# First batch's scores as plain f32 products, and the table of distances scaled on GpSimd

## The chip, the cores and the metric

The kernel runs on one core of a Trainium2 chip. A core has TensorE (matrix products into PSUM), VectorE, ScalarE and GpSimd (elementwise work) and SyncE, whose queue (SP) issues all of this kernel's DMAs. The metric is the device time of one execution in microseconds. Before the change the median of three runs is 654.57 us (652.57 to 655.28).

## What is computed

Windowed attention with a linear bias for 8 batches of 8 heads (576 positions, head width 64), and behind it a mixing layer over positions and channels. Cut to what matters:

```python
scores = scale * np.matmul(q, k.transpose(0, 1, 3, 2))      # scale = 1/8
bias   = slopes[:, None, None] * (-np.abs(rel))[None]       # slopes 2^-(h+1), rel = query - key position
mask   = (rel >= 0) & (rel < 128)
scores = np.where(mask, scores + bias[None], -1e9)
attn   = softmax(scores)
x      = np.matmul(attn, v)                                 # heads side by side: (B, 576, 512)
theta  = x @ w_theta
zr, zi = x * cos(theta), x * sin(theta)
u      = x + w_tok_r @ zr + w_tok_i @ zi                    # over positions
out    = u + relu(u @ w_ch)
```

All arrays are float32.

## The kernel before, in words

The 64 heads are worked in 32 pairs, two heads at a time: head 2p lies in array rows and partitions 0 to 63, head 2p+1 in 64 to 127. Pairs 0 to 3 are batch 0. A pair's scores come in three groups of tiles (`SCORES`): tile 0 alone (both heads' last 64 queries in one product of 192 columns, `mm`), tiles 1 and 2 (128 and 256 columns per head), tiles 3 and 4 (256 and 256 per head, `ps`). Each tile holds only the keys of the window.

To keep f32 precision the kernel splits q and k into a high part of the type f32r and a low rest, also f32r: `split_high` has ScalarE write `qh` (q times a power of two and -1/8) and `kh`; `split_low` has VectorE write `ql` = q - qh and GpSimd `kl` = k - kh. The scores are the sum of three products, qh kh, ql kh and qh kl. `weigh` is one VectorE instruction per tile and head: scores from PSUM times a power of two plus the table of distances (`bands`, a constant from the host with both heads' slopes; the power of two turns it to the pair's slopes), with the row's minimum taken along; ScalarE follows with the exponential in place (`front`, `back`). For the first four pairs (`PLAIN = 4`) the attention weights are turned by TensorE in f32 (`flip`, into PSUM, copied out as `pt` by ScalarE) and multiplied with plain f32 values (`ps<-vb,pt`); from pair 4 on f16 parts and DMA transposes do this.

While the first batch's attention runs (`start`), the weights are unpacked: 4 chunks of w_theta and 9 of w_tok arrive as pairs of 32-bit words (u_hi, u_lo, xtf, z_hi and z_lo are the buffers that they pass through), and `unpack` turns each into high and low parts: ScalarE (`apart`, L168, L169), VectorE (`together`, L174, L176), ScalarE and VectorE again (`split`, and for w_tok a row scale, L181 to L193). `pace` mixes these steps with the scores.

The order on each engine's queue is set by a scheduler that models time and moves instructions within their dependencies; the queues themselves run in order. Buffers come from pools: `qk` has two buffers for each of qh, kh, ql and kl, so a pair's tile reuses the one of the pair two before it. q and k are loaded into `qr` and `kr` (one buffer each); pair 1 borrows a buffer of the values (`vb`). GpSimd clears the unused corner of q's tile first. `prepare(p)` splits pair p-1 and loads pair p.

## Time and profile before

| what | value |
|---|---|
| median of the runs | 654.57 us |
| the profiled execution, its own time | 654.73 us |
| its span, first to last instruction | 652.7 us |
| TensorE busy | 604.9 us (93%) |
| VectorE busy | 529.3 us (81%) |
| ScalarE busy | 499.0 us (76%) |
| GpSimd busy | 145.7 us (22%) |
| mean granted TensorE clock | 0.963 |
| DMA traffic | 79.16 MB, mean 121 GB/s |

In the profile a time is counted from the start of the span. PE is TensorE, DVE VectorE, ACT ScalarE, POOL GpSimd. The share of busy time is a mean over stages of different kinds: the change lies in the first 65 us, and that stage has to be read by itself. A duration in a timeline row can overlap with the next instruction's; what an instruction takes from its engine is the distance from its start to the next start. The granted clock is a share of full speed, 1.00 being 2.4 GHz and 0.50 being 1.2 GHz.

### The profile page before, as it was taken

Reading aid. Unit: us, or ns where it says so; the run is one execution under the profiler, and the core shown is the slowest. Engines: PE = TensorE matmul, PEld = TensorE weight load, DVE = VectorE, ACT = ScalarE, POOL = GpSimd, SP = SyncE. Lnnn points to the kernel's source line nnn. Section 1 sums busy time; section 2 is a strip of 40 time slices with the busy share of each in tenths; the row PEclk is TensorE's granted clock in tenths of the full one; section 3 lists DMA queues with packets and bytes.
Section 4 is the critical chain, followed back from the end, with each engine's and each line's share of the span. In section 5 each row is a group of like instructions: output and inputs, shape, how many; then the busy total and the mean of one; then the engine's idle time right before and its main releaser. Section 6 shows DMA issues by size and latency. Waiting matters only on the chain.

```text
span 652.7 us, 14918 instructions
## 1 busy us (share of the span) xinstructions
PE 604.9 (93%) x5712; PEld 520.5 (80%) x5712; DVE 529.3 (81%) x1313; ACT 499.0 (76%) x945; POOL 145.7 (22%) x196
## 2 busy tenths in 40 slices
PE   4869888689999999999999999999999999999998
PEld 3758666578887898789878887889878988799887
DVE  4998799797799778988799878997899878946612
ACT  6999879785987668976988778786898799727710
POOL 3001001542213202222203302231212212210220
PEclk9567999798999899999999999999999999999999
DMA  9954412996038740698039920887058901631001
GB/s 267 338 176 123 106 25 59 210 200 147 27 79 199 173 109 21 143 199 188 23 75 197 211 70 20 188 176 171 28 104 197 183 28 41 136 83 38 19 19 56
DMA packets 149096, 79.16 MB, mean 121 GB/s; under 512 B 122144, under 2 KB 138528, under 8 KB 149024
## 3 DMA queue, kind: packets, MB, share of 16 engines
q1 hardware_dynamic: 149024, 78.21, 51.6%
q8 instruction: 45, 0.74, 0.5%
q14 instruction: 27, 0.22, 0.1%
HBM read 39.39 MB, written 9.44 MB: 75 GB/s over the span
## 4 chain that ended last, share of the span: by engine, by line
PE 59%; DVE 18%; ACT 12%; DMA 9%; issue 2%; SPq 0%; POOL 0%; ACTq 0%; DVEq 0%; POOLq 0%
PE mm L73 47%; PE ps L73 9%; DMA pt<-hl 7%; PE ps L88 2%; ACT front L436 2%; ACT back L436 2%; DVE hl L452 2%; DMA qr<-in_qt_dram 2%; ACT hl L450 2%; DVE g L568 1%; DVE f L568 1%; DVE x_sb L490 1%; ACT L436 1%; DVE z_lo L513 1%; DVE fixed L141 1%
## 5 line engine op out<-in xcount | busy, mean ns | idle before, releaser
L73 PE MATMUL mm<-wtk_hi,z_lo 128*128 128x288 f16 x576 | 166.2, 289 | 6.4 <-DVE z_lo L513 5.5
L73 PE MATMUL mm<-wtk_hi,z_hi 128*128 128x288 f16 x576 | 166.8, 290 | 0.5 <-ACT z_hi L512 0.5
L73 PE MATMUL mm<-wtk_lo,z_hi 128*128 128x288 f16 x576 | 166.2, 289 | 0.0
L73 PEld LDWEIGHTS <-z_hi 128*128 128x128 f16 x1152 | 108.1, 99 | 31.1 <-ACT z_hi L512 0.8
L642 POOL TENSOR_TENSOR u_lo<-xtf,u_hi 128x288 fp32r<-128x288 f32 x64 | 54.6, 868 | 137.6 <-DVE vl L370 95.2
L349 POOL TENSOR_TENSOR kl<-kr,kh 128x576 fp32r<-128x576 f32 x31 | 44.0, 1418 | 154.6 <-issue 80.7
L73 PEld LDWEIGHTS <-z_lo 128*128 128x128 f16 x576 | 56.9, 99 | 26.0 <-DVE z_lo L513 10.5
L436 ACT ACTIVATE front<-front,fixed 128x256 f32<-128x256 f32 (+2 forms) x160 | 60.4, 444 | 14.2 <-DVE fixed L433 13.9
L73 PE MATMUL ps<-vh,pt 128*128 128x65 f16 x1008 | 54.6, 198 | 12.6 <-DMA pt<-hl 10.6
L73 PEld LDWEIGHTS <-pt 128*128 128x128 f16 x1512 | 52.7, 100 | 15.3 <-DMA pt<-hl 12.8
L452 DVE SCALAR_TENSOR_TENSOR hl<-front,hl 128x1024 f16<-128x1024 f32 x28 | 51.4, 1837 | 9.4 <-ACT hl L450 9.3
L436 ACT ACTIVATE back<-back,fixed 128x256 f32<-128x256 f32 x128 | 57.2, 494 | 0.4 <-DVE fixed L433 0.4
L640 ACT CAST u_hi<-xtf 128x288 fp32r<-128x288 f32 x64 | 27.0, 423 | 38.9 <-DVE xtf L638 38.9
L73 PE MATMUL ps<-vl,pt 128*128 128x64 f16 x504 | 52.3, 196 | 0.0
L73 PE MATMUL mm<-u_hi,wch_hi 128*128 128x288 f32 x256 | 47.9, 309 | 0.0
L433 DVE CUSTOM_DVE_ANT_0 back<-ps,bands 128x256 f32<-128x256 f32 x128 | 46.8, 419 | 1.1 <-PE ps L73 1.1
L638 DVE SCALAR_TENSOR_TENSOR xtf<-mm,fixed,xtf 128x288 f32<-128x288 f32 x64 | 32.4, 509 | 18.8 <-PE mm L73 18.8
L73 PE MATMUL mm<-wth_hi,x_hi 128*128 128x512 f32 x160 | 46.4, 412 | 0.9 <-DVE x_hi L530 0.9
L73 PE MATMUL ps<-kh,qh 64*128 64x256 f32 (+1 forms) x256 | 41.7, 321 | 5.2 <-DVE x_sb L490 3.9
L670 DVE SCALAR_TENSOR_TENSOR xtf<-mm,xtf 128x288 f32<-128x288 f32 x64 | 29.1, 454 | 20.8 <-PE mm L73 20.0
L73 PE MATMUL mm<-u_hi,wch_lo 128*128 128x288 f32 x256 | 44.5, 295 | 0.0
L73 PE MATMUL mm<-u_lo,wch_hi 128*128 128x288 f32 x256 | 44.4, 295 | 0.0
(162 smaller groups left out, 1487.4 us busy)
## 6 DMA issues: line engine op xcount, KB each, us to landing
vb<-in_vx_dram SPq DMA_DIRECT2D x16, 650.0 KB, 5.7
out_dram<-xtf SPq DMA_DIRECT2D x64, 144.0 KB, 1.8
kr<-in_kt_dram SPq DMA_DIRECT2D x31, 288.0 KB, 3.9
qr<-in_qt_dram SPq DMA_DIRECT2D x31, 144.0 KB, 2.9
qr<-in_qt_dram SPq DMA_DIRECT2D x31, 128.0 KB, 3.1
xtf<-in_wch_dram SPq DMA_DIRECT2D x4, 512.0 KB, 4.2
z_hi<-in_wtok_dram SPq DMA_DIRECT2D x2, 576.0 KB, 6.0
z_lo<-in_wtok_dram SPq DMA_DIRECT2D x2, 576.0 KB, 6.2
```

Of the source, the lines that this page charges most:

```text
L73: ins = nc.tensor.matmul(*args, **kw)
L88: ins = nc.tensor.transpose(*args)
L349: rest = nc.gpsimd.tensor_tensor(out=kl, in0=kr, in1=kh.bitcast(F32), op=ALU.subtract)
L433: self.weighed = nc.vector.tensor_tensor_reduce(out=sb, in0=ps, in1=bias, scale=2.0 ** -(2 * self.p % H + 1), scalar=3.0e38, op0=ALU.add, ...
L436: self.exps.append(nc.scalar.activation(sb, sb, AF.Exp, bias=least, scale=-1.0))
L450: self.copied = nc.scalar.activation(hl[:, 0], src, AF.Copy, scale=2.0 ** PEXP)
L452: self.lowered = nc.vector.scalar_tensor_tensor(out=hl[:, 1], in0=src, scalar=2.0 ** PEXP, in1=hl[:, 0], op0=ALU.mult, op1=ALU.subtract)
L568: nc.vector.scalar_tensor_tensor(out=z, in0=x_sb[:, i, :], scalar=zs[:, c:c + 1], in1=z, op0=ALU.mult, op1=ALU.mult)
L638: nc.vector.scalar_tensor_tensor(out=xtf[:, m, cs], in0=y_ps[:, :HALF], scalar=st["back"], in1=xtf[:, m, cs], op0=ALU.mult, op1=ALU.add)
L640: nc.scalar.copy(u_hi[:, m, cs], xtf[:, m, cs])
L642: return nc.gpsimd.tensor_tensor(out=u_lo[:, m, cs], in0=xtf[:, m, cs], in1=u_hi[:, m, cs].bitcast(F32), op=ALU.subtract)
L670: nc.vector.scalar_tensor_tensor(out=xtf[:, e, cs], in0=o_ps[:, :HALF], scalar=0.0, in1=xtf[:, e, cs], op0=ALU.max, op1=ALU.add)
```

## The change

For pairs 0 to 3 q and k are used as they are loaded: four plain f32 buffers per pair (named qh, kh, ql and kl, from the same pool) hold q, k and the table of distances in two pieces (512 and 192 columns). `split_pair` hands them through, and each score product is one f32 product in place of three f32r ones. The factor -1/8 moves into `weigh`, whose power of two for the pair's slopes moves into the table: the host's table is multiplied by -4, pair 0's comes by DMA straight into its buffers, and GpSimd makes the table of pair p from that of pair p-1 by a factor 0.25 (`distances`), and from pair 3's the one that all later pairs use, `bands`, by a factor -16. q's corner is cleared per pair on GpSimd. Pairs 4 and later are computed as before.

```diff
--- before.py
+++ after.py
@@ -127,9 +127,12 @@
     sums, rows, invs, lim = (rings[name].take() for name in ("sum", "row", "inv", "lim"))
 
     qr = const.tile([128, S + 64], F32, name="qr")
-    second = vbp.tile([128, GROUP, NT, 65], F32, name="vb").rearrange("p h c d -> p (h c d)")
-    qr_too, kr_too = second[:, :S + 64], second[:, S + 64:2 * S + 64]
-    for t in [qr, qr_too] + peaks + [front[:, 192:256] for front in fronts]:
+    def plain_buffers():
+
+        return [qk.tile([128, w], F32, name=name) for name, w in (("qh", S + 64), ("kh", S), ("ql", S + 64), ("kl", S))]
+
+    plain = [plain_buffers() for _ in range(2)]
+    for t in [p[0][:, 512:] for p in plain] + [front[:, 192:256] for front in fronts] + peaks + [qr]:
         nc.gpsimd.memset(t, 0.0)
 
     ORDER = (0, 4, 1, 5, 2, 6, 3, 7, 8)
@@ -232,7 +235,13 @@
 
     def load_pair(p):
         b, h = divmod(2 * p, H)
-        q, kr = (qr_too, kr_too) if p == 1 else (qr, ld.tile([128, S], F32, name="kr"))
+        if p < PLAIN:
+            if p >= 2:
+                plain.append(plain_buffers())
+                nc.gpsimd.memset(plain[p][0][:, 512:], 0.0)
+            q, kr = plain[p][:2]
+        else:
+            q, kr = qr, ld.tile([128, S], F32, name="kr")
         nc.sync.dma_start(out=q[:64, :S], in_=qt[b, h])
         nc.sync.dma_start(out=q[64:, :512], in_=qt[b, h + 1, :, :512])
         nc.sync.dma_start(out=q[64:, S:], in_=qt[b, h + 1, :, 512:])
@@ -329,7 +338,17 @@
         nc.vector.tensor_copy(fixed[:, c:c + GROUP], scale[:, 9:13])
 
     def split_pair(p, raw):
-        return split_low(split_high(p, raw))
+        return raw if p < PLAIN else split_low(split_high(p, raw))
+
+    def distances(p):
+
+        if p == 0:
+            nc.sync.dma_start(out=plain[0][2][:, :512], in_=band[:, :512])
+            nc.sync.dma_start(out=plain[0][3][:, :192], in_=band[:, 512:])
+            return
+        parts = (bands[:, :512], bands[:, 512:]) if p == PLAIN else (plain[p][2][:, :512], plain[p][3][:, :192])
+        for to, of in zip(parts, (plain[p - 1][2][:, :512], plain[p - 1][3][:, :192])):
+            nc.gpsimd.tensor_scalar(out=to, in0=of, scalar1=-16.0 if p == PLAIN else 0.25, scalar2=None, op0=ALU.mult)
 
     def split_high(p, raw):
 
@@ -389,6 +408,8 @@
             self.p = p
             self.terms = parts.pop(p)
             self.early = p < PLAIN
+            self.bias = ((plain[p][2], plain[p][3]) if self.early else (bands, bands[:, 512:]))
+            self.scale = -0.125 if self.early else 2.0 ** -(2 * p % H + 1)
             self.heads = [Head(2 * p + e, self) for e in range(2)]
             self.mx = rings["mx"].take().rearrange("p (e i) -> p e i", e=2)
             self.pt, self.exps = {}, []
@@ -396,13 +417,14 @@
 
         def scores(self, tiles, behind=None):
 
-            last = len(self.terms) - 1
+            terms = (self.terms,) if self.early else self.terms
+            last = len(terms) - 1
             if tiles == (0,):
                 _, _, k0, kn, _ = TILES[0]
                 ps = ps_m.tile([128, 512], F32, name="mm")
-                for j, (qm, km) in enumerate(self.terms):
+                for j, (qm, km) in enumerate(terms):
                     mm(ps[:, :kn], qm[:, 512:], km[:, k0:k0 + kn], start=(j == 0), stop=(j == last))
-                self.weigh(0, 0, self.src[0][:, :kn], ps[:, :kn], bands[:, 512:], behind)
+                self.weigh(0, 0, self.src[0][:, :kn], ps[:, :kn], self.bias[1][:, :kn], behind)
                 return
             ps = ps_s.tile([128, 2, 512], F32, name="ps")
             if tiles == (1, 2):
@@ -413,7 +435,7 @@
             off = 0
             for i in tiles:
                 q0, qn, k0, kn, _ = TILES[i]
-                for j, (qm, km) in enumerate(self.terms):
+                for j, (qm, km) in enumerate(terms):
                     for e in range(2):
                         rows = slice(64 * e, 64 * e + 64)
                         mm(ps[:, e, off:off + kn], qm[rows, q0:q0 + qn], km[rows, k0:k0 + kn],
@@ -424,13 +446,13 @@
                 _, _, _, kn, c0 = TILES[i]
                 for e in range(2):
                     sb = sbs[e][:, off:off + kn]
-                    self.weigh(i, e, sb, ps[:, e, off:off + kn], bands[:, 256 * e + c0:256 * e + c0 + kn], behind)
+                    self.weigh(i, e, sb, ps[:, e, off:off + kn], self.bias[0][:, 256 * e + c0:256 * e + c0 + kn], behind)
                 off += kn
 
         def weigh(self, i, e, sb, ps, bias, behind):
 
             least = self.mx[:, e, i:i + 1]
-            self.weighed = nc.vector.tensor_tensor_reduce(out=sb, in0=ps, in1=bias, scale=2.0 ** -(2 * self.p % H + 1),
+            self.weighed = nc.vector.tensor_tensor_reduce(out=sb, in0=ps, in1=bias, scale=self.scale,
                                                           scalar=3.0e38, op0=ALU.add, op1=ALU.min, accum_out=least)
             with tc.issue_after(behind.ins) if behind is not None else nullcontext():
                 self.exps.append(nc.scalar.activation(sb, sb, AF.Exp, bias=least, scale=-1.0))
@@ -758,8 +780,9 @@
 
         next(load)
         prepare(0)
-        nc.sync.dma_start(out=bands, in_=band)
+        distances(0)
         prepare(1)
+        distances(1)
         last = None
         for p in range(H // 2 + 1):
             new = Pair(p)
@@ -790,6 +813,8 @@
             if p in (1, 2):
                 measure(p - 1, peaks[0][:, GROUP * (p - 1):GROUP * p])
             prepare(p + 2)
+            if 2 <= p + 2 <= PLAIN:
+                distances(p + 2)
             last = new
         for _ in load:
             pass
@@ -850,7 +875,7 @@
     split = np.where((rel >= 0) & (rel < WINDOW), rel.astype(np.float32), np.float32(-NEG * 256))
     half = split * 0.5
     last = np.concatenate([split[:64, :192], half[:64, :192]], axis=0)
-    return np.concatenate([split, half, last], axis=1).astype(np.float32)
+    return (-4.0 * np.concatenate([split, half, last], axis=1)).astype(np.float32)
 
 
 def _layout(q, k, v, moe_w_theta, moe_w_tok_r, moe_w_tok_i, moe_w_ch):
```

On TensorE, from the second turning of pair 0's weights (back) to the products with pair 0's values (vb,pt); ps and mm are products in PSUM, L88 is a turning, L73 a product, + is the changed kernel and - the one before:

```order
 L88 MATMUL ps<-fixed,back 128x128 x8
+L73 MATMUL ps<-kh,qh 128x256 x4
+L73 MATMUL ps<-vb,pt 128x65 x18
 L73 MATMUL mm<-kh,qh 128x192
-L73 MATMUL mm<-kh,ql 128x192
-L73 MATMUL ps<-kh,qh 128x256 x2
-L73 MATMUL ps<-kh,ql 128x256 x2
-L73 MATMUL ps<-kl,qh 128x256 x2
-L73 MATMUL ps<-kh,qh 128x256 x2
-L73 MATMUL ps<-kh,ql 128x256 x2
-L73 MATMUL ps<-kl,qh 128x256 x2
-L73 MATMUL mm<-kl,qh 128x192
```

Two f32 products per head stand for six f32r ones, and the values of pair 0 now come ahead of pair 2's tile 0 (mm).

On GpSimd, from the last fill ahead of the loop to the first fills of vh (the values' parts), before:

```order
L133 MEMSET front_102 128x64
L369 MEMSET vh 128x5
L349 TENSOR_TENSOR kl<-kr,kh 128x576
L349 TENSOR_TENSOR kl<-vb,kh 128x576
L349 TENSOR_TENSOR kl<-kr,kh 128x576 x4
L369 MEMSET vh 128x5 x4
```

and in the changed kernel, where ql and kl of pairs 1 to 3 are the two pieces of the table and the qh fills are the corners of q for pairs 2 and 3:

```order
L388 MEMSET vh 128x5
L351 TENSOR_SCALAR ql<-ql 128x512
L351 TENSOR_SCALAR kl<-kl 128x192 x2
L241 MEMSET qh 128x128
L351 TENSOR_SCALAR ql<-ql 128x512
L351 TENSOR_SCALAR kl<-kl 128x192
L351 TENSOR_SCALAR bands<-kl 128x192
L241 MEMSET qh 128x128
L351 TENSOR_SCALAR ql<-ql 128x512
L351 TENSOR_SCALAR bands<-ql 128x512
L368 TENSOR_TENSOR kl<-kr,kh 128x576 x2
```

Four subtractions of 576 columns give way to eight scalings, six of them behind pair 1's own two.

On the SP queue, from the second chunk of w_tok to the fourth (z_lo to u_lo), before, where the q and k in qr and kr are pair 3's:

```order
L158 DMA z_lo<-in_wtok_dram 128x1152
L245 DMA vb<-in_vx_dram 128x4x325
L253 DMA vb<-in_vx_dram 128x4x325
L158 DMA u_hi<-in_wtok_dram 128x1152
L158 DMA u_lo<-in_wtok_dram 128x1152
L236 DMA qr<-in_qt_dram 64x576
L237 DMA qr<-in_qt_dram 64x512
L238 DMA qr<-in_qt_dram 64x64
L239 DMA kr<-in_kt_dram 128x576
```

and in the changed kernel, where qr and kr are pair 4's and qh and kh pair 2's:

```order
L254 DMA vb<-in_vx_dram 128x4x325
L245 DMA qr<-in_qt_dram 64x576
L246 DMA qr<-in_qt_dram 64x512
L247 DMA qr<-in_qt_dram 64x64
L246 DMA qh<-in_qt_dram 64x512
L245 DMA qh<-in_qt_dram 64x576
L247 DMA qh<-in_qt_dram 64x64
L248 DMA kh<-in_kt_dram 128x576
L248 DMA kr<-in_kt_dram 128x576
L262 DMA vb<-in_vx_dram 128x4x325
L161 DMA u_hi<-in_wtok_dram 128x1152
L161 DMA u_lo<-in_wtok_dram 128x1152
```

The loads of pairs 2 and 4 stand ahead of these two chunks now; before, pair 2's stood ahead of xtf, z_hi and z_lo, and pair 4's far behind.

## Rows read from the trace of the kernel before

**Rows 1.** Busy time by stretch (window: length, busy us per engine, clock, DMA share, GB/s).

```profile
20.00:30.00 10.00, 9.52 (x47) 8.89 (x48) 9.86 (x28) 10.00 (x21) 1.42 (x1) 0.50 1.05 354
30.00:40.00 10.00, 6.56 (x35) 6.11 (x36) 9.74 (x20) 10.00 (x21) 1.46 (x1) 0.50 0.47 145
40.00:50.00 10.00, 7.04 (x43) 6.21 (x40) 9.55 (x30) 10.00 (x21) 0.88 (x1) 0.67 0.55 197
50.00:60.00 10.00, 9.15 (x61) 8.59 (x62) 9.07 (x27) 10.00 (x22) 0.67 (x1) 0.69 0.58 174
```

**Rows 2.** Timeline of ScalarE (start us, us, engine, line, operation, out<-in, shape, count).

```profile
12.32 0.69 ACT L168 ACTIVATE u_lo<-u_lo 128x512 f32<-128x512 f32 x1
...
14.46 0.66 ACT L168 ACTIVATE xtf<-xtf 128x512 f32<-128x512 f32 x1
...
15.59 0.49 ACT L436 ACTIVATE front<-front,fixed 128x256 f32<-128x256 f32 x1
...
31.41 0.72 ACT L168 ACTIVATE u_lo<-u_lo 128x576 f32<-128x576 f32 x1
...
32.65 0.73 ACT L340 ACTIVATE qh<-qr 128x640 fp32r<-128x640 f32 x1
...
33.84 0.78 ACT L192 ACTIVATE wtk_hi<-z_hi,fixed 128x576 f16<-128x576 f32 x1
```

**Rows 3.** Timeline of the SP queue, loads of weight chunks.

```profile
7.09 0.33 SPq L158 DMA_DIRECT2D u_lo<-in_wth_dram  x1
7.68 0.33 SPq L158 DMA_DIRECT2D xtf<-in_wth_dram  x1
...
19.31 0.34 SPq L158 DMA_DIRECT2D u_lo<-in_wtok_dram  x1
```

**Rows 4.** DMA issues up to 90 us: count, KB each, us to landing.

```profile
xtf<-in_wth_dram SPq DMA_DIRECT2D x2, 512.0 KB, 6.6
...
u_lo<-in_wtok_dram SPq DMA_DIRECT2D x1, 576.0 KB, 10.1
...
u_lo<-in_wth_dram SPq DMA_DIRECT2D x1, 512.0 KB, 5.2
```

**Rows 5.** Timeline of VectorE.

```profile
12.15 0.29 DVE L433 CUSTOM_DVE_ANT_0 front<-ps,bands 128x128 f32<-128x128 f32 x1
...
19.80 0.82 DVE L347 SCALAR_TENSOR_TENSOR ql<-qr,qh 128x640 fp32r<-128x640 f32 x1
20.53 0.28 DVE L433 CUSTOM_DVE_ANT_0 front<-ps,bands 128x128 f32<-128x128 f32 x1
...
34.21 1.95 DVE L347 SCALAR_TENSOR_TENSOR ql<-qr,qh 128x640 fp32r<-128x640 f32 x1
36.08 0.75 DVE L176 SCALAR_TENSOR_TENSOR u_lo<-u_lo 128x576 int32<-128x576 int32 x1
```

**Rows 6.** Timeline of GpSimd.

```profile
2.26 0.30 POOL masks.py:199 TENSOR_SCALAR_AFFINE_SELECT fixed<-fixed 128x128 f32<-128x128 f32 x1
...
11.96 1.51 POOL L349 TENSOR_TENSOR kl<-vb,kh 128x576 fp32r<-128x576 f32 x1 [3.22 <-ACT kh L341]
...
34.02 1.46 POOL L349 TENSOR_TENSOR kl<-kr,kh 128x576 fp32r<-128x576 f32 x1 [11.84 <-ACT kh L341]
```

**Rows 7.** GpSimd's groups by form (busy us, mean ns of one, idle before).

```profile
L642 POOL TENSOR_TENSOR u_lo<-xtf,u_hi 128x288 fp32r<-128x288 f32 x64 | 54.6, 868 | 137.6 <-DVE vl L370 95.2 <-ACT u_hi L640 35.2 <-ACT vh L368 3.7
...
L197 POOL TENSOR_TENSOR wch_lo<-xtf,wch_hi 128x512 fp32r<-128x512 f32 x4 | 5.4, 1343 | 4.7 <-ACT wch_hi L196 4.7
...
L133 POOL MEMSET qr<- 128x640 f32 x1 | 0.6, 637 | 0.0
```

**Rows 8.** Timeline of TensorE.

```profile
22.43 0.58 PE L73 MATMUL ps<-kh,qh 64*128 64x256 f32 x2
...
24.01 0.53 PE L73 MATMUL mm<-kl,qh 128*128 128x192 f32 x1
24.86 7.94 PE L73 MATMUL ps<-vb,pt 128*128 128x65 f32 x36 [0.32 <-ACT pt L445]
```

## The prediction, made before the changed kernel ran

> **What bounds the kernel now.** I read the core's summary first, then busy time in stretches of 10 us, then the timelines of ScalarE, VectorE, GpSimd, TensorE and the SP queue up to 80 us, because the diff touches only the first batch's four pairs. In the four stretches from 20 to 60 us ScalarE is busy 10.00 of 10 each time and VectorE 9.86, 9.74, 9.55 and 9.07, so VectorE has 1.78 us of idle time in 40; TensorE has 7.73 us and GpSimd nearly all of it [rows 1]. The stretch is an exchange between two full engines: ScalarE and VectorE unpack the 13 weight chunks and, between them, weigh the scores and take the exponentials of pairs 0 to 4. TensorE has slack there, although its clock was granted at 0.50 to 0.69. Whatever comes off both full engines comes off the end of the stretch, and everything later shifts with it: from the first token mixing on, no engine's order changes. So the whole question is how much of the first 65 us goes.
>
> **The change part by part.**
> ScalarE loses qh and kh of four pairs. Pair 3's two stand from 32.65 to 33.84, so 1.19 us a pair and 4.76 us in all [rows 2].
>
> Not all of that is gained. The first two weight chunks behind pair 1's loads are taken as they land: u_lo is issued at 7.09 and takes 5.2, so it lands at 12.29, and ScalarE starts on it at 12.32; xtf lands at 7.68 + 6.6 = 14.28 and is started at 14.46 [rows 2 to 4]. These loads don't come sooner (the table of distances is now two transfers, which puts them one issue later if anything). With 2.38 us of copies gone before 14.46, ScalarE can only bring forward one exponential of 256 columns, which stood behind xtf at 15.59 (0.49 us), and the 0.18 us to the landing [rows 2]. That is 0.67 of 2.38; 1.71 us turn into waiting. ScalarE's net is 4.76 - 1.71 = 3.05 us.
>
> VectorE loses ql of four pairs. Pairs 0 and 1 come while it still waits for weight chunks to land, and count as nothing. Pair 2's costs 20.53 - 19.80 = 0.73, pair 3's 36.08 - 34.21 = 1.87, together 2.60 us [rows 5].
>
> Pair 3's is that long because GpSimd was writing kl from 34.02 to 35.48 [rows 6]: the VectorE instruction began at 34.21 and ended 0.68 us after GpSimd did, that is, it stood until GpSimd was through. Weighing, which takes its scores from PSUM, does not stand: at 12.15, inside kl of pair 1 (11.96, 1.51 us), it took its usual 0.29 [rows 5, 6]. The Trainium skill has this as a rule ("SBUF — State Buffer", section "Who interferes with whom"): a VectorE instruction with two SBUF inputs and a GpSimd instruction that reads SBUF exclude each other for the whole instruction, one with at most one SBUF input is free. The trace agrees in both halves, with the 1.87 and the 0.29. By that rule the new scalings, which read SBUF, stop VectorE just as kl did, and with every one of them stopping it the VectorE term below would be 2.60 - 3.12, a small loss instead of a small gain.
>
> GpSimd loses four kl and gains four scalings of 512 columns and four of 192, two of them for pair 1, before VectorE is busy; the other six fall between 15 and 30 us. No row shows a scaling. From below, by a plain fill of 640 columns in 0.637 us, about 1.0 ns a column, 512 and 192 columns cost 0.51 and 0.19, six of them 2.1 us. From above, by two-operand subtractions, 1.343 for 512 columns and 0.868 for 288 (more than 192 can cost), they cost 6.6 us [rows 7]. The nearest row is the one-operand select of 128 columns, 0.30 us [rows 6]; with the fill's 1.0 ns for further columns that gives 0.68 and 0.36, 3.12 us for six, which I take. VectorE reads two SBUF operands in about two thirds of this stretch, my estimate, so 2.0 of 3.12 stop it. VectorE's net is 2.60 - 2.0 = 0.6 us.
>
> TensorE does one f32 product in place of three f32r ones. The only plain f32 products in the trace are those with the values: 18 of them appear as 36 weight loads and products in 7.94 us at the half clock, 0.221 us each [rows 8]. A pair's scores are 9 products, so 18 of these: 3.97 us at the half clock, if the columns (65 there, up to 256 here) add nothing. With three f32r parts two tiles of 256 columns take from 22.43 to 24.01, 1.58 us, so a pair some 3.9 [rows 8]. From below the change is then about nothing. From above, with time in proportion to columns, one f32 product part of 256 columns would take 0.221 x 256/65 = 0.87 us and a pair some 13.4, 9.5 more. I take +0.5 us a pair, near the lower end, because in the nearest products of the same shape the two heads (array rows 0 to 63 and 64 to 127) run side by side: 12 parts of 256 columns in that 1.58 us, 0.13 each, where one alone would need more. TensorE's 7.73 us of idle time hide it; without that cover it costs 2 us. The skill states ("FP8 and Floating Point Precision", section "TensorE Precision Notes") that true f32 takes four passes. No run here separates passes; by four in place of three a pair would take an estimated 1.3 us more at the half clock, and 3 pairs in that clock 3.9, still inside the idle time.
>
> The waits that are added: TensorE starts on pair 0 when q and k land, not after ScalarE's copy, which helps by under 1 us and then waits for the table. GpSimd's fills of the q tiles for pairs 2 and 3 now stand behind scalings that wait for VectorE's weighing, and the SP queue's loads stand behind those fills: pair 3's load holds back the two xtf chunks. Those are needed only after 35 us, so I cost that at nothing.
>
> **Sum.** ScalarE could end 3.05 us earlier, VectorE 0.6. Neither can run ahead of the other for long, since each chunk passes back and forth between them; I take the middle, 1.8 us. The profiled execution took 654.73, 0.16 above the median of 654.57. Forecast: 654.57 - 1.8 = 652.8 us, with a range of its own from 654.0 (0.6) to 651.5 (3.05).
>
> **Rivals.**
> A, more is gained. Pair 2's q and k no longer stand ahead of the first unpacking loads, so chunks land sooner, and the scalings fall beside weighing, which they don't stop. Then ScalarE's 4.76 us count nearly whole: 650.2. For it speaks ScalarE's zero idle time in rows 1; against it, that u_lo and xtf are still the first loads behind pair 1's.
> B, f32 products of 64 rows don't run side by side. Pairs 1 to 3 in the cold clock each need 16 more part times of 0.221, 3.5 us, together 10.6; half of it covered by TensorE's idle time, 5.3 stays: 654.6 - 1.8 + 5.3 = 658.1. The f32r rows speak against it.
> C, the change of places in the SP queue eats the gain. Pair 4's q and k (576 KB) now go out ahead of the second round of weight loads. At the 354 GB/s of 20 to 30 us that is 1.7 us; u_lo, issued at 19.31 and 10.1 us on its way, landed at 29.41 and was used at 31.41 [rows 1 to 4]. Now it lands near 31.1, while ScalarE wants it some 2 us sooner than before. It waits 1.7 us, and what is left is about nothing: 654.4.
> D, slower through GpSimd. If the six scalings cost what two-operand subtractions do, 6.6 us, and all stop VectorE, it loses 6.6 - 2.6 = 4.0, of which its 1.78 us of idle time hide part: 654.6 + 2.2 = 656.8. It decides from the point where the blocked time exceeds 2.60 + 1.78 = 4.4 us. That the rule on shared access holds in this trace speaks for it; that a scaling reads one operand, against it.
>
> **How the numbers follow.** Forecast 0.46, A 0.20, C 0.18, D 0.10, B 0.06. Half a per cent, about what a measurement can tell from no change, is 3.3 us: faster is below 651.3, slower above 657.8. Faster: most of A and the edge of the forecast, 0.22. Slower: B and a third of D, with what I have not seen, 0.11. The rest, 0.67, is within. The range takes in most of A and up to D: 650.0 to 656.6.
>
> **What would show it.** Right: ScalarE busy under 10 of 10 between 10 and 20 us, with waits for the landing of u_lo and xtf; scalings of 512 columns near 0.7 us with VectorE's two-operand rows stretched beside them; the last exponentials of pair 3 some 2 us sooner; nothing different after the first token mixing but the shift. A pair's 256-column tile near 0.9 us at the half clock or 0.45 at the full one says that the heads run side by side; twice that is B. A wait of ScalarE for u_lo near 30 us is C. I am wrong in the mechanism if ScalarE and VectorE gain idle time of over 4 us between 20 and 60 us and TensorE is what they wait for.

## Result: slower by 0.8%, and where in the profile it stands

The changed kernel takes 659.48 us (median of 20 runs, 654.83 to 661.39) against 653.03 us of the kernel before in as many runs beside it. The medians stand 6.4 us apart; the ratio, which goes by the means, is 1.0084 (5.5 us), with a 95% interval of 1.0065 to 1.0104. The forecast was 652.8 us. The profiled execution took 659.62 us, its span is 657.8. In the runs further down, single executions of over 2500 us count in a median and not in a ratio.

Busy time by stretch, the kernel after (columns as in [rows 1]):

```profile
10.00:20.00 10.00, 7.06 (x36) 5.08 (x35) 7.67 (x26) 8.74 (x18) 5.97 (x7) 0.82 1.03 385
20.00:30.00 10.00, 8.56 (x40) 7.34 (x38) 10.00 (x29) 8.48 (x19) 2.12 (x2) 0.50 1.04 300
30.00:40.00 10.00, 9.21 (x40) 7.33 (x41) 9.55 (x28) 9.86 (x18) 1.51 (x2) 0.50 0.94 309
40.00:50.00 10.00, 8.57 (x48) 8.08 (x49) 9.83 (x22) 10.00 (x22) 1.55 (x1) 0.67 0.35 107
50.00:60.00 10.00, 7.72 (x34) 5.38 (x32) 8.15 (x29) 10.00 (x22) 0.00 (x0) 0.50 0.47 150
60.00:70.00 10.00, 9.02 (x43) 9.03 (x44) 5.01 (x13) 3.48 (x8) 1.57 (x4) 0.50 0.22 61
```

Up to 60 us it reads much as forecast: ScalarE has some idle time ahead of 40 us, VectorE gains little. The row that is new is the last. ScalarE is busy for 3.48 of 10 us, TensorE for 9.02, at a granted clock of 0.50. Before, the same stretch had ScalarE at 8.40 and the clock at 1.00:

```profile
60.00:70.00 10.00, 8.65 (x86) 7.80 (x84) 7.37 (x35) 8.40 (x18) 1.53 (x4) 1.00 0.21 60
```

ScalarE's timeline names what it waits for; after first, then before:

```profile
61.76 1.72 ACT L458 ACTIVATE back<-back,fixed 128x256 f32<-128x256 f32 x4
70.66 1.01 ACT L467 COPY pt<-ps 128x1024 f32<-128x1024 f32 x1 [7.18 <-PE ps L88]
```

```profile
62.39 1.70 ACT L436 ACTIVATE back<-back,fixed 128x256 f32<-128x256 f32 x4
65.69 1.01 ACT L445 COPY pt<-ps 128x1024 f32<-128x1024 f32 x1 [1.60 <-PE ps L88]
```

ScalarE ends pair 3's exponentials at 63.48 instead of 64.09, so 0.6 us of the gain did reach this point. Then it waits 7.18 us for TensorE's turning of pair 3's probabilities, where it waited 1.60. TensorE's timeline from there, after:

```profile
42.53 6.92 PE L73 MATMUL ps<-vb,pt 128*128 128x65 f32 x36 [1.43 <-ACT pt L467]
...
51.68 1.65 PE L73 MATMUL ps<-kh,qh 64*128 64x128 f32 x8
55.43 1.97 PE L88 MATMUL ps<-fixed,back 128*128 128x128 f32 x8 [2.10 <-ACT pt L467]
57.33 2.08 PE L73 MATMUL ps<-kh,qh 64*128 64x256 f32 x8
59.34 0.47 PE L88 MATMUL mm<-fixed,peak 128*128 128x128 f32 x1
60.98 7.94 PE L73 MATMUL ps<-vb,pt 128*128 128x65 f32 x36 [1.16 <-DVE fixed L455]
68.71 1.91 PE L88 MATMUL ps<-fixed,front 128*128 128x128 f32 x8
```

And before:

```profile
46.34 7.95 PE L73 MATMUL ps<-vb,pt 128*128 128x65 f32 x36 [2.70 <-DVE fixed L433]
54.08 1.91 PE L88 MATMUL ps<-fixed,front 128*128 128x128 f32 x8
...
58.03 1.09 PE L88 MATMUL ps<-fixed,back 128*128 128x128 f32 x8 [0.60 <-ACT pt L445]
...
60.54 4.23 PE L73 MATMUL ps<-vb,pt 128*128 128x65 f32 x36
64.61 1.04 PE L88 MATMUL ps<-fixed,front 128*128 128x128 f32 x8
```

At 55.43 the changed kernel is 2.6 us ahead (the back turning began at 58.03 before). Then the same 36 rows of pair 2's values take 7.94 us instead of 4.23, and the turning 1.91 instead of 1.04. Both go with the clock. Busy time in stretches that are all at one clock, before and then after:

```profile
47.00:56.00 9.00, 9.00 (x45) 9.00 (x44) 7.65 (x13) 9.00 (x19) 1.55 (x1) 0.50 0.55 170
57.00:95.00 38.00, 32.34 (x228) 26.74 (x226) 31.27 (x87) 30.55 (x57) 1.53 (x4) 1.00 0.29 69
```

```profile
45.00:73.00 28.00, 24.74 (x118) 22.15 (x119) 20.08 (x61) 20.82 (x44) 3.11 (x5) 0.50 0.31 97
75.00:84.00 9.00, 5.19 (x48) 4.75 (x45) 4.95 (x13) 5.69 (x9) 0.00 (x0) 1.00 0.34 65
85.00:87.00 2.00, 2.00 (x5) 1.61 (x6) 1.98 (x4) 1.81 (x4) 0.00 (x0) 0.50 1.00 164
```

Before, the clock rose to 1.00 (2.4 GHz) at 56.3 us, after ten microseconds in which TensorE did not pause. In the changed kernel it stayed at 0.50 (1.2 GHz) until 74.4 and fell again from 84.6 to 88.0, in the first theta products. (The instants are read from windows of 1 us.)

From pair 2's values to the first mixing product (91.77 before, 100.81 after) the 9.0 us come together as follows, each the difference of two distances between starts: start of the values 0.4 (60.98 against 60.54); the values 3.7; from there to pair 3's values 1.7; to the first theta product 1.8; the theta products 1.4. The third, fourth and fifth follow from starts at 64.61, 70.05 and 77.29 before and 68.71, 75.82 and 84.91 after. Second and third stand at half clock but for the end of the third, and the last has its first 3.1 us there; together they are 6.8 us. The fourth stands at full clock and is a wait for VectorE, 3.27 us where it was 1.03:

```profile
83.66 0.77 PE L88 MATMUL ps<-fixed,x_sb 128*128 128x128 f32 x5 [3.27 <-DVE x_sb L512]
```

The two profiled executions differ by 4.9 (the medians by 6.4), so some 4 of the 9.0 are given back later: before has three later spells at half clock, from 121.1, 148.4 and 213.3 us, 13.6 us in all; after has one, from 129.0, of 6.8. The lower clock is not one of the profiled execution alone: over the changed kernel's 20 runs the mean granted clock is 0.944 to 0.958 (median 0.950), in the kernel before's runs beside the experiments 0.955 to 0.992 (medians 0.963 to 0.976).

### The profile page after: what moved, and what is told of

Read it like the earlier page. It is cut to its first block, busy times and chain, and to the rows that moved or that the text cites. A ratio compares the mean times of both kernels' runs of the same rounds, so it can differ in the third digit from the quotient of the medians.

```text
span 657.8 us, 14837 instructions
## 1 busy us (share of the span) xinstructions
PE 610.6 (93%) x5676; PEld 523.1 (80%) x5676; DVE 525.4 (80%) x1309; ACT 494.4 (75%) x937; POOL 148.6 (23%) x203
## 4 chain that ended last, share of the span: by engine, by line
PE 63%; DVE 14%; ACT 11%; DMA 10%; issue 2%; POOL 0%; SPq 0%; ACTq 0%; POOLq 0%; DVEq 0%
PE mm L73 49%; PE ps L73 11%; DMA pt<-hl 6%; PE ps L88 3%; ACT back L458 2%; DVE hl L474 2%; ACT front L458 2%; ACT hl L472 1%; DVE g L590 1%; DVE f L590 1%; DMA u_lo<-in_wtok_dram 1%; DVE z_lo L535 1%; ACT L458 1%; DVE fixed L144 1%; DMA kr<-in_kt_dram 1%
## 5 line engine op out<-in xcount | busy, mean ns | idle before, releaser
L73 PE MATMUL mm<-wtk_hi,z_lo 128*128 128x288 f16 x576 | 165.0, 287 | 6.5 <-DVE z_lo L535 5.5
L73 PE MATMUL mm<-wtk_hi,z_hi 128*128 128x288 f16 x576 | 165.4, 287 | 0.5 <-ACT z_hi L534 0.5
L73 PE MATMUL mm<-wtk_lo,z_hi 128*128 128x288 f16 x576 | 164.9, 286 | 0.0
L73 PEld LDWEIGHTS <-z_hi 128*128 128x128 f16 x1152 | 107.3, 98 | 30.3 <-ACT z_hi L534 0.8
L664 POOL TENSOR_TENSOR u_lo<-xtf,u_hi 128x288 fp32r<-128x288 f32 x64 | 53.4, 850 | 139.6 <-DVE vl L389 81.4
L73 PEld LDWEIGHTS <-z_lo 128*128 128x128 f16 x576 | 56.4, 98 | 25.4 <-DVE z_lo L535 10.5
L368 POOL TENSOR_TENSOR kl<-kr,kh 128x576 fp32r<-128x576 f32 x28 | 39.7, 1418 | 132.0 <-issue 80.6
L73 PE MATMUL ps<-vh,pt 128*128 128x65 f16 x1008 | 53.3, 196 | 11.8 <-DMA pt<-hl 10.2
L73 PEld LDWEIGHTS <-pt 128*128 128x128 f16 x1512 | 51.4, 99 | 14.6 <-DMA pt<-hl 12.1
L73 PE MATMUL ps<-kh,qh 64*128 64x256 f32 (+1 forms) x288 | 49.5, 374 | 5.7 <-DVE fixed L455 3.8
L73 PE MATMUL ps<-vl,pt 128*128 128x64 f16 x504 | 51.0, 194 | 0.0
L73 PE MATMUL mm<-wth_hi,x_hi 128*128 128x512 f32 x160 | 47.3, 418 | 1.0 <-DVE x_hi L552 1.0
L73 PE MATMUL mm<-u_hi,wch_hi 128*128 128x288 f32 x256 | 47.8, 308 | 0.0
L73 PE MATMUL mm<-u_hi,wch_lo 128*128 128x288 f32 x256 | 44.5, 295 | 0.0
L73 PE MATMUL mm<-u_lo,wch_hi 128*128 128x288 f32 x256 | 44.4, 295 | 0.0
L73 PE MATMUL mm<-wth_lo,x_hi 128*128 128x512 f32 x160 | 44.3, 399 | 0.0
```

The lines of the kernel that those rows point to most:

```text
L73: ins = nc.tensor.matmul(*args, **kw)
L368: rest = nc.gpsimd.tensor_tensor(out=kl, in0=kr, in1=kh.bitcast(F32), op=ALU.subtract)
L664: return nc.gpsimd.tensor_tensor(out=u_lo[:, m, cs], in0=xtf[:, m, cs], in1=u_hi[:, m, cs].bitcast(F32), op=ALU.subtract)
```

## Experiments

Theory 1: the loss is TensorE's clock in this tail. Theory 2: it is GpSimd's scalings, or the loads that now wait on SP's queue. Each run has the kernel before beside it on the same chip, but the runs come from several chips, so rows are compared by their ratios rather than their medians; "half clock" sums the time at 0.50 in the first 100 us of its profile, "values" is the start and length of pair 2's.

| run | half clock | values | first mixing product | median | ratio, 95% interval |
|---|---|---|---|---|---|
| before | 34.2 | 60.54, 4.23 | 91.77 | 653.03 | |
| after | 58.0 | 60.98, 7.94 | 100.81 | 659.48 | 1.0084 (1.0065, 1.0104) |
| e1_f32_only | 40.9 | 62.21, 4.23 | 94.96 | 652.03 | 0.9989 (0.9966, 1.0012) |
| e2_f32r_still | 68.4 | 62.37, 7.95 | 105.29 | 664.77 | 1.0179 (1.0147, 1.0211) |
| e3_warm | 54.5 | 60.12, 5.76 | 95.78 | 656.12 | 1.0057 (1.0027, 1.0087) |
| e4_no_scalings | 58.0 | 59.72, 7.94 | 99.84 | 658.30 | 1.0080 (1.0053, 1.0107) |
| e5_warm_more | 30.6 | 59.27, 4.23 | 91.41 | 652.41 | 0.9994 (0.9974, 1.0014) |
| e6_three_plain | 64.9 | 63.09, 8.05 | 103.45 | 665.66 | 1.0202 (1.0179, 1.0225) |
| e7_gpsimd_loads | 37.6 | 61.67, 4.23 | 94.43 | 654.10 | 1.0023 (0.9999, 1.0046) |
| e8_both | 40.9 | 65.35, 4.15 | 97.42 | 658.86 | 1.0107 (1.0080, 1.0135) |
| e12_before_hole | 44.4 | 63.88, 4.23 | 94.36 | 654.69 | 1.0054 (1.0021, 1.0088) |
| five14 | 51.2 | 60.67, 7.08 | 98.06 | 657.90 | 1.0094 (1.0059, 1.0128) |
| tail13 | 32.7 | 59.48, 4.23 | 91.34 | 651.07 | 0.9969 (0.9950, 0.9987) |
| before15 | 40.9 | 62.49, 4.13 | 95.17 | 656.78 | 1.0060 (1.0038, 1.0082) |

**The plain f32 product alone.** The kernel before, with the f32 product in `scores`:

```diff
+            if self.early:
+                qh, kh = self.terms[0]
+                self.terms = ((qh.bitcast(F32), kh.bitcast(F32)),)
```

> The kernel before, with pairs 0 to 3's scores as one plain f32 product of qh and kh instead of three f32r products; every split is still made, and the low parts are left out of these pairs' scores. TensorE does what it does in the changed kernel; ScalarE, VectorE, GpSimd and SP's queue do what they do before. Theory 1 (the loss is TensorE's granted clock: 0.50 from 43.7 to 74.4 us in the changed kernel, from 46.0 to 56.3 before): slower than before by 3 to 6 us, 656 to 659 us, pair 2's values of x36 at 7.9 us as in the changed kernel and not 4.2. Theory 2 (GpSimd's six scalings and the loads behind them on SP's queue make the loss): within 1 us of before, 652 to 654 us, values of pair 2 at 4.2 us.

652.03 us, level with the kernel before, as theory 2 had it; pair 2's values at 62.21 take 4.23. Theory 1 as first put, that f32 score products keep the clock low, is out: TensorE had the changed kernel's products, and the clock rose at 58.8, after a stretch like that of before:

```profile
47.42 7.94 PE L73 MATMUL ps<-vb,pt 128*128 128x65 f32 x36 [1.09 <-ACT pt L448]
55.16 1.91 PE L88 MATMUL ps<-fixed,front 128*128 128x128 f32 x8
...
58.04 1.30 PE L73 MATMUL ps<-kh,qh 64*128 64x128 f32 x8 [0.38 <-DVE fixed L183]
59.26 1.10 PE L88 MATMUL ps<-fixed,back 128*128 128x128 f32 x8
```

The last row starts with no wait; after the change this turning has 2.10 us of waiting for ScalarE ahead of it.

**The f32r products, with the rest of the change.** A constant tile takes the place of q and k:

```diff
-            terms = (self.terms,) if self.early else self.terms
+            terms = (None,) * 3 if self.early else self.terms     # None: still[:, :128], still[:, :kn]
```

> The changed kernel, with pairs 0 to 3's scores as three f32r products of one constant tile, as many and as wide as before the change; what it leaves out is q and k themselves in these scores. TensorE does what it does before; loads, scalings and the missing splits are the changed kernel's. Theory 1 (clock): the full clock is back by about 57 us, pair 2's values take about 4.2 us, and the time is at or under the kernel before, 649 to 653 us. Theory 2 (scalings and queue): still slow, 657 to 660 us.

664.77 us, the other way from what theory 1 said. With f32r products the clock stays low even longer. So f32r score products alone do not bring the clock back. TensorE's waits are there, too:

```profile
45.57 7.95 PE L73 MATMUL ps<-vb,pt 128*128 128x65 f32 x36 [2.47 <-ACT pt L475]
...
58.34 1.60 PE L88 MATMUL ps<-fixed,back 128*128 128x128 f32 x8 [1.93 <-DVE fixed L463]
...
62.37 7.95 PE L73 MATMUL ps<-vb,pt 128*128 128x65 f32 x36 [0.85 <-ACT pt L475]
```

The clock did rise, at 55.3, and fell at 58.7, behind the wait of 1.93 us.

**No scalings.** All pairs share one table:

```diff
-        for to, of in zip(parts, ...):
-            nc.gpsimd.tensor_scalar(out=to, in0=of, scalar1=..., op0=ALU.mult)
+            nc.sync.dma_start(out=bands[:, :512], in_=band[:, :512])       # p == 0 only
```

> The changed kernel without GpSimd's scalings of the table: pairs 0 to 3 and all later ones share one table, loaded once; what it leaves out is the pairs' own slopes (and the sign of the scores) in pairs 0 to 3. Theory 1 (clock): little changes, 657 to 660 us, pair 2's values still at 7.9 us. Theory 2 (about 7 us of scalings on GpSimd): 652 to 654 us.

658.30 us, ratio 1.0080 (1.0053 to 1.0107) against 1.0084: the scalings are not the loss.

**Work put into TensorE's waits.** `warm(n)` issues n products nobody reads, behind the last TensorE instruction:

```diff
+    def warm(n):
+        ps = ps_m.tile([128, 512], F32, name="mm")
+        with tc.issue_after(latest_pe[0].ins):
+            for k in range(n):
+                mm(ps, wth_hi[:, k % 4, :128], wth_hi[:, (k + 1) % 4, :], start=(k == 0), stop=(k == n - 1))
                 scores(SCORES[1])
+                if p == 3:
+                    warm(5)
                 last.flip(1)
                 scores(SCORES[2])
+                if p == 3:
+                    warm(3)               # e5_warm_more: 7, and warm(2), (3), (3) later
```

> The changed kernel with eight added f32r products (128x512 of wth_hi by itself, thrown away) on TensorE: five behind pair 3's front scores, where it waited 2.10 us for ScalarE's copy, three behind pair 3's back scores, where it waited 1.16 us. At half clock they fill about 2.1 and 1.3 us, so they cost at most about 0.5 us by themselves. Theory 1 (clock, and that gaps and f32 work keep it low): the clock rises to 1.00 before 66 us, pair 2's values take under 6 us, and the time falls by 3 to 6 us, to 653 to 656 us. Theory 2: within 1 us of the changed kernel, 658 to 661 us.

> The changed kernel with twenty thrown-away f32r products (128x512 of wth_hi by itself) in TensorE's waits of the first batch's tail: five behind pair 3's front scores, seven behind its back scores, two ahead of pair 3's values, three and three in the waits before the first theta products. With eight of them the clock was 1.00 from 55.3 to 62.8 us, fell in pair 2's values and came back at 72.6, and the time was 3.4 us under the changed kernel's. Theory 1 (the loss is TensorE's granted clock in this tail): with the clock at 1.00 from about 55 on, pair 2's values take 4.2 us, the first mixing product starts at 91 to 93 us (100.8 in the changed kernel, 91.8 in the kernel before), and the time is 651 to 654 us. Theory 2 (the loss is the load order: pair 2's and 3's loads wait on SP's queue and hold back the weight chunks): the clock's part is spent with eight products, 655 to 657 us.

Eight gave 656.12: the clock rose at 55.7, fell at 62.6 and caught the second half of the values (5.76 us). Twenty gave 652.41, level with the kernel before, and by the ratios 0.9% (5.9 us) under the changed kernel, though TensorE does more:

```profile
59.27 4.23 PE L73 MATMUL ps<-vb,pt 128*128 128x65 f32 x36 [0.54 <-ACT pt L475]
```

This run shows that the clock in this tail is the loss: loads, scalings and every other engine's work are the changed kernel's. Besides the fill the scheduler has moved a few instructions, above all pair 4's tile 0, three f32r products with 0.86 us on TensorE and one exponential with 0.35 us on ScalarE, from 50.82 us to behind the added products (58.25). The run does not show whether it is the closed waits or the kind of the added products that brought the clock back.

**Three plain pairs.**

```diff
+WHOLE = 3
-        if p < PLAIN:                      # load_pair, split_pair, distances, bias, scale, terms
+        if p < WHOLE:
```

> The changed kernel with plain f32 scores and scaled tables in pairs 0 to 2 alone; pair 3 is split and scored by three f32r products as before. ScalarE gets back one pair's two splits (about 1.2 us of its 4.76 saved). Theory 1 as put first (f32 score products in the tail keep the clock low): pair 2's values at 4.2 us and 651 to 654 us. Theory 1 as it stands after the run with f32 products alone, which was level with the kernel before (it is TensorE's gaps around 50 to 60 us that decide, not the kind of product): anything from 652 to 659 us, by whether the clock rises before 61 us; a kernel with the rise is within 2 us of the kernel before, one without is 4 to 7 us above it. Theory 2 (load order): about 657 us either way, since pair 2's load still waits on SP's queue.

665.66, worse than either bound. Pair 3's f32r products did not bring the clock back: it stayed at 0.50 from 36.4 to 77.4, with TensorE waiting 2.91, 1.47 and 1.57 us ahead of its rows at 44.59, 57.98 and 63.09. Why the loss is larger than the 4 to 7 us expected stays open.

**The loads of pairs 2 and 3 on GpSimd's queue.**

```diff
+        queue = nc.gpsimd if 2 <= p < PLAIN else nc.sync
-        nc.sync.dma_start(out=q[:64, :S], in_=qt[b, h])        # and the other three
+        queue.dma_start(out=q[:64, :S], in_=qt[b, h])
```

> The changed kernel with pairs 2's and 3's loads issued by GpSimd instead of SP, so that their wait for the buffers of pairs 0 and 1 no longer holds back the weight chunks behind them on SP's queue (u_hi's load went out at 24.7 us in the changed kernel, 17.7 before). Theory 1 (clock): ScalarE's two waits of 0.76 us near 26 and 29 us go, the tail still stands at half clock, 656 to 660 us. Theory 2 (load order): 652 to 655 us.

> The changed kernel with both edits: the twenty thrown-away products in TensorE's waits and pairs 2's and 3's loads issued by GpSimd. Theory 1: 650 to 653 us, at or just under the kernel before. Theory 2: the same as the run with GpSimd's loads alone. If both terms are real, this is the fastest of the four and may pass the kernel before.

654.10, as theory 2 said; but not by the way that was expected. The weight chunk u_hi goes out at 21.2 instead of 24.7, yet ScalarE still waits, 1.26 us at 21.2, 1.20 at 28.3 and 1.47 at 32.1, the last for u_hi itself. What differs is again the tail: TensorE now waits 4.74 us once, ahead of pair 1's values at 47.33, runs on from there, and the clock rises at 58.1. So the two theories meet here: the place of the loads changes where TensorE waits, and this run doesn't rule out that it is where the tail's waits come from. Both edits together should then have been fastest. They gave 658.86: five products at half clock took 2.50 us, and pair 2's values began at 65.35. Filling is free only where there is a wait.

**A pause put into the kernel before.**

```diff
+                    for k in range(9):
+                        pause = nc.gpsimd.memset(idle, 0.0)    # the first waits for pair 1's values
+                    held.append(pause)                         # pair 2's front turning waits for the last
                 last.flip(0)
```

> The kernel before, with nothing taken away, and a pause of about 2 us put into TensorE's dense stretch: the turning of pair 2's front probabilities (54.1 us) waits for nine small memsets on GpSimd that start when pair 1's values end. By itself a pause there costs 1 to 2 us, less what TensorE waits behind it anyway (0.60 and 0.25 us). Theory 1 (a gap in the dense stretch keeps the clock at half): no rise at 56 us, pair 2's values at 7.9 us instead of 4.2, and 656 to 661 us, as the changed kernel. If gaps don't matter: 653.5 to 655 us, values at 4.2 us.

```profile
46.13 7.94 PE L73 MATMUL ps<-vb,pt 128*128 128x65 f32 x36 [2.03 <-DVE fixed L437]
...
57.45 1.97 PE L89 MATMUL ps<-fixed,front 128*128 128x128 f32 x8 [2.68 <-POOL idle L780]
...
63.88 4.23 PE L73 MATMUL ps<-vb,pt 128*128 128x65 f32 x36
```

By its time, 654.69, and by values of 4.23 this is the other branch ("if gaps don't matter"), and theory 1's number is missed. Its mechanism is borne out in part: behind the pause (2.68 us) the clock stayed at 0.50 past 56, to 62.3. The pause also put the turning off by 3.4 us (57.45 for 54.08), which is less than the 6.0 us that the rise moved. Pair 2's values came at 63.88, behind the rise, and the first mixing product 2.6 us later than before, about the pause itself. Here a later rise cost nothing more, because the long products stood behind it.

**Other uses of the products.** Three more runs had the twenty products or a part of them.

> The kernel before with the same twenty thrown-away products at the same places of the program: the change at an equal clock is the run e5_warm_more against this one. Before already has the clock at 1.00 from 56.3 to 120 us, so theory 1 (clock) expects little: 651 to 654 us, and e5_warm_more, 652.4, within 1 us of it: the change by itself is then worth nothing that can be measured. If ScalarE's saved splits show once the clock is equal, this one is over 1.5 us slower than e5_warm_more.

> The changed kernel with the twenty products (652.4 us), and the second weight chunk's load put ahead of pair 1's q and k on SP's queue (it went out at 7.8 us and its pass on ScalarE began at 13.1). If ScalarE's early waits (3.85, 1.48, 1.57 and 0.36 us ahead of 11.6) are where the saved splits went, the chunk's first two passes fill part of them, and the time falls by 0.5 to 1.5 us, to 651 to 652 us; if the loads bind as a whole (the DMA engines' share is 1.03 from 10 to 30 us), no change; if the clock falls differently, up to 657.

> The changed kernel with pairs 2's and 3's loads issued by GpSimd (654.1 us; its clock rose at 58.1 us and fell again from 78.6 to 82.0, in the first theta products), and of the thrown-away products only the eight from pair 3's values on: two ahead of them, three and three ahead of the theta products. Theory 1 (clock): the fall at 78.6 goes, about 1.6 us less: 651.5 to 653.5 us. Otherwise 654 to 655 us.

They gave 656.72 (ratio 1.0061, 1.0037 to 1.0085), 654.74 (1.0034, 1.0004 to 1.0064) and 654.20 (1.0027, 0.9996 to 1.0057). The first is a miss, as the products cost the kernel before 4.7 us; TensorE's waits there are short, 0.60 and 0.25 us. The earlier load did not help: VectorE was late with x_sb, TensorE waited 4.91 us at 53.4, and the clock was at 0.50 from 51.8 to 58.6. In the third the fall at 78.6 went, without a gain in the time: the first mixing product came at 94.31 instead of 94.43.

**Twelve products, none near the scales.** As above with `warm(5)`, `warm(7)` alone; the same in the kernel before; the five alone; and three more ahead of the theta products.

> The changed kernel with twelve thrown-away products: five behind pair 3's front scores and seven behind its back scores, none later, so that the chain of the scales stands where it does in the changed kernel. Clock theory: full clock from 54 to 56 us on, pair 2's values at 4.2 us, with or without a short fall near 80; if the forecast gain of 1.8 us is real once the clock is there, 650 to 652.5 us, under the kernel before; if the change is worth nothing at equal clock, 652.5 to 654.

> The kernel before with the same twelve products at the same two places. Its clock rises at 55 to 56 us anyway, so the clock theory expects no gain; five products ahead of the back turning, where TensorE waits 0.60 us, and seven where it waits about 0.25 us, at full clock cost 1.2 and 1.7 us less these waits, if nothing else hides them: 653 to 656 us. Equal clock and equal products: if the forecast gain is real, tail13 is under this one by 1.5 us or more.

> The changed kernel with only the five products behind pair 3's front scores, at the wait of 2.10 us. If this wait alone keeps the clock down, the clock rises near 54 to 56 us and stays through pair 2's values: 652 to 655 us. With five and three products it rose at 55.7 and fell again at 62.6, in the values (656.1 us); if the second wait (1.16 us) matters too, the same again: 655 to 658 us.

> As tail13, with three more products between the eight turnings of x_sb and the first theta product, where TensorE waits 0.5 to 0.9 us. If tail13's clock falls in the first theta products (3.4 us at half, as in the changed kernel and four others), it doesn't here: 1 to 1.6 us under tail13. If tail13 has no fall there, no difference.

tail13 is the fastest kernel of all: 651.07 us (649.06 to 652.54), with an interval under 1, so it beats the changed kernel and, narrowly, the kernel before. Its rows for ScalarE and TensorE:

```profile
60.53 1.71 ACT L466 ACTIVATE back<-back,fixed 128x256 f32<-128x256 f32 x4
63.10 0.46 ACT L466 ACTIVATE front<-front,fixed 128x192 f32<-128x192 f32 x1 [0.86 <-DVE fixed L463]
64.63 1.01 ACT L475 COPY pt<-ps 128x1024 f32<-128x1024 f32 x1 [1.07 <-PE ps L89]
```

```profile
52.09 2.19 PE L73 MATMUL mm<-wth_hi 128*128 128x512 f32 x5
54.52 1.09 PE L89 MATMUL ps<-fixed,back 128*128 128x128 f32 x8 [0.23 <-ACT pt L475]
...
56.72 1.88 PE L73 MATMUL mm<-wth_hi 128*128 128x512 f32 x7
...
59.48 4.23 PE L73 MATMUL ps<-vb,pt 128*128 128x65 f32 x36 [0.46 <-ACT pt L475]
```

The clock rose at 53.8 and pair 3's exponentials end at 62.24, 1.85 us before the kernel before's 64.09; 0.35 us of that is pair 4's tile 0, whose exponential stands behind them here (63.10) and ahead of them before (58.56). The five alone were not enough (657.90): the clock rose at 54.8, TensorE then waited 2.77 us ahead of the values, and it fell at 61.6, inside them. So filling the first wait was not enough. The same twelve cost the kernel before 4.4 us; that pair of runs therefore doesn't isolate the change. Three more products (652.01, 1.0003, 0.9979 to 1.0028) add nothing that can be measured, although the first mixing product came at 90.10. This run and e5_warm_more, which hold the same twelve products, are level with the kernel before, so the gain over it rests on tail13 alone.

## Why the prediction was wrong, step by step

**The step that failed** is "Whatever comes off both full engines comes off the end of the stretch, and everything later shifts with it", with the remark ahead of it that TensorE has slack there "although its clock was granted at 0.50 to 0.69". ScalarE's part did end 0.61 us sooner, but it no longer set the end: ScalarE then waited 7.18 us for TensorE. The prediction took the low clock of [rows 1] for a fixed condition, and its sum had no term for TensorE's waits but their length and none for the clock behind them. "TensorE's 7.73 us of idle time hide it" held for the length of the f32 products, as e1_f32_only is level with the kernel before.

The order on ScalarE's queue changed with the edit, too. Its copy ahead of pair 1's values stands at 41.49 us instead of 46.16, far more than the 1.20 us of other work that ScalarE is ahead by 40 us. So TensorE starts these values at 42.53 instead of 46.34 and is through with the next products at 53.33, before ScalarE has worked off the weights ahead of its copy of pair 2's front probabilities; this copy in the changed kernel, and in the kernel before:

```profile
54.37 1.00 ACT L467 COPY pt<-ps 128x1024 f32<-128x1024 f32 x1
```

```profile
56.99 0.99 ACT L445 COPY pt<-ps 128x1024 f32<-128x1024 f32 x1
```

It comes 3.2 us behind the end of the turning that it copies, before 1.0. A wait of 2.10 us opens there and one of 1.16 behind it, the clock does not come back at 56, and pair 2's values, turnings and the first theta products pay half clock.

That the tail's loss is this clock is shown: the same rows stand at both levels, and the runs with products in the waits took the loss away. What keeps the clock low is not. The stretch ahead of the 2.10 us is no shorter than that before: TensorE ran from 42.53 to 53.33 without a pause, at 0.50 from 43.7, against 46.34 to the rise at 56.3. In e5_warm_more it ran from 41.42 without a pause, and the clock rose only at 54.0, 1.4 us into the added products. Waits and the kind of products are not told apart by these runs, the order of the queues was never held fixed, and why three plain pairs cost more than four stays open, too.

**ScalarE's term.** Removed copies worth 4.76 us, 1.71 of it turned into waiting. Ahead of 31 us ScalarE now waits in these rows (after):

```profile
5.87 0.66 ACT L171 ACTIVATE u_hi<-u_hi 128x512 f32<-128x512 f32 x1 [3.85 <-DMA u_hi<-in_wth_dram]
...
8.56 0.63 ACT L202 ACTIVATE wth_hi<-u_hi 128x512 fp32r<-128x512 f32 x1 [1.48 <-DVE u_hi L179]
10.76 0.46 ACT L458 ACTIVATE front<-front,fixed 128x192 f32<-128x192 f32 x1 [1.57 <-DVE fixed L455]
...
26.72 0.68 ACT L184 ACTIVATE z_hi<-z_hi 128x576 f32<-128x576 f32 x1 [0.76 <-DVE z_hi L179]
...
29.85 0.78 ACT L195 ACTIVATE wtk_hi<-z_hi,fixed 128x576 f16<-128x576 f32 x1 [0.76 <-DVE fixed L186]
```

By 40 us it has done 30.20 us of work against 33.76 before (sums of 10-us windows), 3.56 less, while all 4.76 us of copies are gone: 1.20 us of other work are ahead, and 3.56 went into waits for loads and for VectorE, twice the 1.71. Of these, 1.04 is the first chunk alone, issued at 0.74 us in both kernels and used at 5.87 instead of 4.83; in five variants of the changed kernel (e4, e5, five14, tail13, theta16) it was used at 4.88 to 5.71, so that part varies from one execution to the next. The first exponential starts at 10.76 instead of 11.79, the chunk u_lo at 13.13 instead of 12.32 [rows 2]. Of 3.05 forecast, 0.61 is there at 63.48.

**The middle, 1.8 us.** Near in size once the clock is back: tail13's exponentials end 1.85 us early, 1.5 without pair 4's tile 0, and its median is 1.3 us under the kernel before, by the ratio 0.8 to 3.3. That it is so near is luck in part: it was the middle of 3.05 and 0.6, and of ScalarE's 3.05 the changed kernel shows 0.61.

**The f32 product.** Right. A row of two 256-column tiles with both heads at half clock (after):

```profile
22.13 2.08 PE L73 MATMUL ps<-kh,qh 64*128 64x256 f32 x8 [1.44 <-DVE fixed L455]
```

That is 1.04 us a tile, against "near 0.9", where [rows 8] had 1.58 us for two: the heads run side by side, 0.5 us a pair more, and rival B is out.

**GpSimd's term.** Its price was too low. GpSimd's groups by form, after (columns as in [rows 7]):

```profile
L351 POOL TENSOR_SCALAR ql<-ql 128x512 f32<-128x512 f32 x3 | 5.3, 1768 | 14.2 <-DVE fixed L455 7.4 <-DMA ql<-in_band_dram 6.8
L351 POOL TENSOR_SCALAR bands<-ql 128x512 f32<-128x512 f32 x1 | 1.5, 1492 | 0.1
L351 POOL TENSOR_SCALAR bands<-kl 128x192 f32<-128x192 f32 x1 | 0.7, 691 | 0.1
```

1.49 us for 512 columns and 0.69 for 192 where I took 0.68 and 0.36; that is over the two-operand subtraction's 1.343 [rows 7], the bound from above. It hardly reached VectorE. Beside the scalings at 16.56 and 28.08 (1.87 and 1.94 us instead of 1.49) two of its rows are longer:

```profile
17.00 1.10 DVE L177 SCALAR_TENSOR_TENSOR xtf<-xtf 128x512 int32<-128x512 int32 x1
...
28.59 0.57 DVE L320 TENSOR_SCALAR peak<-peak 128x8 f32<-128x8 f32 x1
```

They took 0.68 and 0.17 in the run without scalings, so 0.8 us together, not 2.0. Rival D had the price right, even low, and the consequence wrong; the run without scalings says what it cost, 1.2 us by the medians and 0.3 by the ratios, neither clear of the noise. The Trainium skill ("SBUF — State Buffer", section "Who interferes with whom"), which the prediction used, calls the port pair that VectorE shares with GpSimd "an exclusive lock". This trace does not bear that out for the scalings, as far as GpSimd's rows can be trusted: VectorE's two-operand row at 17.00 lies within the scaling from 16.56 to 18.43, with about 0.4 us lost on each side, and one at 29.07, within the scaling from 28.08 to 30.02, takes its usual 0.68. The row at 28.59, which is stretched, reads one operand, and the prediction held those for free.

**SP's queue.** Rival C was real in its first half: u_hi's second load went out at 24.74 instead of 17.67 and u_lo's at 25.26 instead of 19.31 [rows 3], because pair 2's loads wait ahead of them. u_lo was used at 32.79 instead of 31.41 [rows 2]. ScalarE's work was rearranged around it, so that no wait of ScalarE names that load. The prediction put the loads that stand behind pairs 2's and 3's at nothing. That is not shown: with these pairs' loads on GpSimd's queue (e7_gpsimd_loads) the kernel is level with the one before (1.0023, 0.9999 to 1.0046), and the clock came back at 58.1.

**The test for a wrong mechanism** looked at 20 to 60 us. ScalarE's idle time there is 1.66 us (0 before), VectorE's 2.47 (1.78 before), so the two gained 2.35, under the 4 us named; the wait for TensorE came at 63.5. The test had the right engine and a stretch that ended too early.

## What to carry to other kernels

In this kernel a clock at 0.50 in a stretch bound elsewhere was not a condition to work with but a state with an end, and where it ended (56.3 us before, 74.4 after) set the price of what followed. Before moving work off an engine that feeds TensorE, find in the trace where the clock rises, ask whether the move puts new waits ahead of that place, and price the next long products at both levels (7.94 and 4.23 us here). If it does, a few unread products in the new waits can be worth trying; in the kernel before, where the waits were short, the same twelve cost 4.4 us.

## What was not expected of the hardware

TensorE ran without a wait from 60.98 to 74.27 us in the changed kernel, mostly f32 products of 65 columns, and the granted clock stayed at 0.50 until 74.4, behind f32r products and a turning. A one-operand GpSimd scaling of 512 f32 columns took 1.49 us, more than a two-operand subtraction of as many (1.343). Taking work from the busiest engine made the kernel 0.8% slower, though the work that it added, f32 products on TensorE and scalings on GpSimd, is not what cost it; and twelve products more, which nobody reads, made that kernel 1.1% faster again (ratios 1.0084 and 0.9969).
